# Sums of four of v moved from TensorE to GpSimd in a planned attention and MoE kernel, and a later due time for the second batch's units

## The chip, the cores and the metric

One core of one Trainium2 chip runs the whole program. The metric is the device time of one execution in microseconds (us), as the median of several runs. Lower is better.

## The reference

q, k and v are (8 batches, 8 heads, 576 rows, 64 columns). For each batch and head there are two attentions, whose results are added:

```
q_d, k_d, v_d = means of 4 neighbouring rows of q, k, v     # 144 rows
out_up    = repeat(softmax(q_d @ k_d.T / 8) @ v_d, 4 times each row)
out_local = softmax(mask(|i - j| < 4, q @ k.T / 8)) @ v
x   = (out_up + out_local), as 4608 tokens of 512 numbers
h   = x @ w_in                       # 512 -> 2048
out = (h * clip(h + 3, 0, 6) / 6) @ w_out
```

So before the large matrix products can use a batch, the kernel needs that batch's sums of four rows of v: 144 of them for each head, 128 from v's first 512 rows and 16 from its last 64.

## The kernel before

**Units.** A unit is two heads of one batch (128 columns), so a batch `b` has four units, numbered `hp` 0 to 3. A unit loads q and k, has them transposed, sums groups of four (`pool4`, L323), makes the scores of both attentions (`scores_d` L419, `scores` L601), the two softmaxes (maximum L470, subtraction L473, exponential L463 and L476, sum L479, reciprocal L485, normalisation `norm` L487 to L492), transposes the weights (`trans_d` L496 with L501, `trans` L632 with L638), copies them out of PSUM (L120 on ScalarE, L122 on VectorE) and multiplies with v (`pv_d` L575 with L586 and L589, `pv` L646 with L656). Normalisation is usually GpSimd's.

**Chunks.** The tokens go through the two large products in chunks (`PART`): 512 tokens first, then 256, then 384 at a time. For each of 16 blocks `f` of the hidden width a first product (`gemm1`, L934) is followed by an activation (ScalarE L940, VectorE L944), a split into two rounded halves (L948, L952) and a second product (`gemm2`, L986). x itself is split in two halves too (L122 or L120, then L837). Chunk 0 is batch 0's first 512 rows; chunk 1 is the rest of batch 0 and the start of batch 1; chunk 2 is all batch 1.

**Batch 0 is direct.** For `b == 0` (`direct`) both attentions are accumulated in PSUM, in two banks for each unit, and x is split straight out of these banks. All of batch 0's banks (`s`) come from six. Its q and k are transposed on TensorE (L274). Each unit's first 512 rows of v arrive in one load (`ld4(0)`, L362), and `sum_pe(0)` (L386) sums them by four matmuls with the identity matrix into one bank (L393); a copy (`evict_v`, L395, by L120 or L122) takes the sums to SBUF. The last 64 rows are summed by one matmul with a 0/1 matrix (L391). Batch 1 (`alone` but not `direct`) already has the first 512 rows summed by `sum4` (L370): one reduction on VectorE (L376), or two additions on GpSimd (L378, L379).

**Weights.** The weights come as 64-bit numbers and are made into two rounded float halves, with ScalarE (L180, L195, L201), VectorE (L185, L189) and either VectorE or GpSimd (L205); a weight's load is L169.

**The order.** All operations are entered into a planner (`Plan`), which simulates the engines at assumed costs before anything is emitted. Each operation has a due time `late`, worked back from deadlines; an engine that is free takes the ready operation with the earliest `late` whose buffers and banks are free. The result is one fixed order for each engine and for SP's queue of loads. `on("sum4", 1.0)` offers VectorE at 1.03 us and GpSimd at 1.3 us, and `PEN["sum4"]` counts GpSimd's offer as due 10 us sooner. Where the planner sees TensorE idle ahead of the first large product, it puts in matmuls that compute nothing (`busy`, L1033, with L1038).

The due time of a batch's units comes from

```
def need(b):
    return start_of(need_chunk(b)) - (EARLY * TC if b and b % 2 == 0 else 0.0) - SLACK[min(b, 3)]
```

and each earlier unit of batch 1 is due 22 (`UNIT_T[1]`) sooner than the next. Everything that batch 1's units do (loads L311, transposes L318, `pool4` L327 or L331 and L333, and all that follows) inherits its `late` from there.

Of the kernel before, what the change touches and what calls it, by code (L numbers as in the profile page):

```python
# [56 lines left out]
def tile_local_down_attention_moe(ctx, tc, q_all, k_all, v_all, _qk_loc, _v_loc, w_in, w_out, ident_d, _mask_d, out):  # L57
# [26 lines left out]
    op = plan.op  # L84
# [74 lines left out]
    def plan_weights(n, keys, after, gate):  # L159
# [43 lines left out]
        def lo(eng):  # L203
# [5 lines left out]
               for i in range(nk)]  # L209
        a = op("ACT", 0.2 + cols / 1070, rebias, lds, take=[place], lag=LAGW)  # L210
        c = op("ACT", 0.2 + cols / 1070, low, lds, lag=LAGW)
        b = op("DVE", 0.2 + cols / 930, partial(bits, 0), [a, c], lock=not by_bank)
# [22 lines left out]
    def plan_duo(b, d, masked):  # L235
# [50 lines left out]
        for u in range(2):  # L286
            unit = plan_unit(b, d, u, row0, k0, kv, PS, qk, evicts, users, masked, early_user, due - (1 - u) * unit_time(b))
            next(unit)
            units.append(unit)
            if b < ALONE or len(units) > 1:  # L290
                next(units.pop(0), None)
# [4 lines left out]
    def plan_unit(b, d, u, row0, k0, kv, PS, duo, evicts, users, masked, early_user, due):  # L296
        hp = 2 * d + u
        row0 = row0 + u * S
        un = b, hp
# [3 lines left out]
        alone = b < ALONE  # L303

        direct = b == 0
# [29 lines left out]
        for kind, t in (("q", q_all), ("k", k_all)):  # L335
# [3 lines left out]
            else:  # L339
                rk = "raw" + k0, hk  # L340
                l = op("SP", 2.0, partial(ldt, t, kind), loads if b == 1 else [], take=[rk], size=dma(4 * S, 128), nd=4)
# [59 lines left out]
        lv, sums = [], []  # L401
# [4 lines left out]
        for g in range(2):  # L406
            rk = ("raw4", ("v", un)) if b == 0 else ("raw" + k0, ("v", un, g))
            l = op("SP", 0.5, partial(ld4, g), take=[rk], size=dma(P, 512) if alone and g else dma((P, NAR)[g], 2048), nd=1 if alone else 1 + g)
            if b == 0:
                loads.append(l)  # L410
            if b == 0 or alone and g:
                bk = PS, ("v4", un, g)
                a = early_user(op("PE", 0.21 if g else 0.86, partial(sum_pe, g), [l], take=[bk], free=[rk], lag=LAGT, rec=2 if g else 8))
                sums.append(early_user(op(on("ev", ROW), 0, partial(evict_v, g), [a], take=[("vd" + k0, un)], free=[bk])))
            else:
                sums.append(op(on("sum4", 1.0), 0, partial(sum4, g), [l], take=[("vd" + k0, un)], free=[rk]))


        def scores_d():  # L419
# [275 lines left out]
        else:  # L695
# [3 lines left out]
                take=[bk, pk, sk] + bks + [pl, sl], lag=LAGT, rec=52)  # L699
# [20 lines left out]
        if alone:  # L720
            subs = []
            for g in range(2):
                a = op("DVE", 0.45, lambda g=g: top(rows(g), greatest(g)), [sl_op])
                subs.append(op("DVE", 0.45, lambda g=g: minus(nc.vector, st["p"][:, :, g], rows(g), greatest(g)), [a],
                               free=[bks[g]]))
# [41 lines left out]
        else:  # L767
            rk = "qk", ("rd", un)
# [7 lines left out]
        else:  # L776
            a = op("PE", 1.4, pv_all, t + lv + turned_d + sums, take=bks + [ok] + xbs,
                   free=[tk, vk, tk_d, ("vd" + k0, un)], lag=LAGT, rec=52)
# [280 lines left out]
    for n in range(len(PART)):  # L1059
        while duos and (need_chunk(duos[0][0]) == n or units):  # L1060
            b, d = duos.pop(0)
# [9 lines left out]


T0, TC, TF, LAG = 55.0, 82.0, 5.1, 2
UNIT_T, EARLY, SLACK = (4.0, 22.0, 20.0, 30.0), 0.7, (4.0, 40.0, -5.0, 28.0)
PRE, GATE = 4, 14

AHEAD = 2
# [14 lines left out]
LAGT = 0.5  # L1092

LAGW = 2.0
ORDERED = ("raw", "qk", "qkd", "v", "vd", "P", "Pd", "Pl", "PT", "rl", "od", "p4", "st", "a", "o0", "o1", "o2", "o3")
HOP, FREE = 0.1, 0.1

# [96 lines left out]
def on(what, size):  # L1194

    return {e: (a + b * size, PEN[what].get(e, 0.0)) for e, (a, b) in COST[what].items()}
# [19 lines left out]
def dma(packets, size):  # L1216

    return packets * (6.5 + 0.049 * size) / 16e3 if size > 256 else packets * (1.3 + 0.13 * size) / 16e3


class Plan:
# [5 lines left out]
    def op(self, eng, cost, fn, after=(), take=(), free=(), size=0, dl=None, lag=0.0, lock=False, rec=0, nd=1, kind=None):  # L1227
        o = Op(len(self.ops), eng, cost, fn, take, size, dl)
        o.kind = kind

        o.rec, o.nd = rec, nd
        o.lag, o.lock = lag, {True: ("DVE", "POOL"), False: ("POOL",)}[lock]
        self.ops.append(o)
        for a in after:
            self.dep(o, a)
        for r in free:
            self.free_after(r, [o])
        return o
# [28 lines left out]
    def emit(self, warm, last, busy):  # L1267
# [30 lines left out]

        turn = {key: [] for key in ORDERED}

# [214 lines left out]
```

## Time and profile before

| what | us |
|---|---|
| median of 3 runs | 946.02 |
| lowest and highest of them | 945.36 and 947.41 |
| the profiled execution's own time | 944.02 |
| its span, first to last instruction | 942.2 |
| TensorE busy in the span | 931.6 |
| VectorE, ScalarE, GpSimd busy | 554.2, 363.2, 298.8 |

PE is TensorE's matmuls, PEld its weight loads, DVE is VectorE, ACT ScalarE, POOL GpSimd, SPq the queue in which SyncE issues transfers. Each engine runs its instructions in the emitted order, and waits at the first that isn't ready. In the timelines the time in brackets is how long the engine stood idle before that row, and for whom it waited.

### The profile page before, as it was taken

To read this page: it belongs to the slowest core of one execution; us is meant where nothing else is said; L and a number is where in the kernel's file an instruction comes from. 1 tells how busy PE (TensorE), PEld (TensorE's weight loads), DVE (VectorE), ACT (ScalarE), POOL (GpSimd) and SP (SyncE) were. 2 spreads that over 40 slices of the span, in tenths; PEclk is the share of its full clock that TensorE was granted. 3 is DMA by queue.
4 is the path that set the end of the run, shared out by engine and by line. 5 is a ranking of instruction groups with operands and counts; after the bars stand their busy time and mean duration, and the time that the engine had idled before them with its cause. 6 is when DMAs were issued, how large, how long until landed. Compare 5 with 4: busy or idle time off the path is not lost.

```text
span 942.2 us, 19819 instructions
## 1 busy us (share of the span) xinstructions
PE 931.6 (99%) x7567; PEld 808.5 (86%) x7567; DVE 554.2 (59%) x1045; ACT 363.2 (39%) x899; POOL 298.8 (32%) x386
## 2 busy tenths in 40 slices
PE   8999999999999999999999999999999999999997
PEld 5677778988889898889889888988988988998996
DVE  7888886477677566554456667555455654323322
ACT  5787755334333334333233333333233432221222
POOL 4345361244462334332325244225125320000000
PEclk9999999999999999999999999999999999999999
DMA  7999353355666565545135555645154520100101
GB/s 210 228 293 288 72 118 64 70 105 119 126 134 132 104 117 113 100 84 114 34 80 122 102 104 102 134 98 97 40 99 80 115 55 12 34 1 2 33 1 33
DMA packets 311758, 93.52 MB, mean 99 GB/s; under 512 B 251376, under 2 KB 297840, under 8 KB 311664
## 3 DMA queue, kind: packets, MB, share of 16 engines
q1 hardware_dynamic: 311376, 91.83, 43.8%
q8 instruction: 59, 0.97, 0.4%
q10 hardware_dynamic: 288, 0.43, 0.2%
q14 instruction: 35, 0.29, 0.1%
HBM read 69.60 MB, written 22.61 MB: 98 GB/s over the span
## 4 chain that ended last, share of the span: by engine, by line
PE 90%; SPq 4%; DMA 3%; DVE 1%; issue 1%; ACT 1%; POOL 0%; DVEq 0%; ACTq 0%
PE h L934 40%; PE o L986 39%; PE a L656 2%; PE a L615 2%; PE a L442 1%; PE a L986 1%; PE a L570 1%; SPq L311 1%; DMA rows<-in_k_dram 1%; DMA arena<-in_v_dram 1%; SPq L548 1%; PE a L428 1%; SPq L522 1%; SPq L527 1%; DMA arena<-in_q_dram 0%
## 5 line engine op out<-in xcount | busy, mean ns | idle before, releaser
L934 PE MATMUL h<-rounded,wp 128*128 128x384 f32 (+2 forms) x2240 | 420.1, 336 | 0.2 <-DVE arena L944 0.2
L986 PE MATMUL o<-wp,rounded 128*128 128x512 f32 x1680 | 408.1, 394 | 0.0
L934 PEld LDWEIGHTS h<-rounded,wp 128*128 128x128 f32 x2240 | 384.1, 188 | 15.1 <-issue 2.7
L986 PEld LDWEIGHTS o<-wp,rounded 128*128 128x128 f32 x1680 | 311.0, 188 | 66.1 <-issue 4.4
L940 ACT ACTIVATE arena<-h 128x384 f32<-128x384 f32 (+2 forms) x192 | 93.7, 490 | 365.6 <-PE h L934 364.7
L944 DVE SCALAR_TENSOR_TENSOR arena<-arena,h 128x384 f32<-128x384 f32 (+2 forms) x192 | 105.1, 547 | 183.0 <-ACT arena L940 181.8
L948 ACT CAST rounded<-arena 128x384 fp32r<-128x384 f32 (+2 forms) x192 | 98.2, 512 | 119.2 <-DVE arena L944 118.7
L952 DVE TENSOR_TENSOR rounded<-arena,rounded 128x384 fp32r<-128x384 f32 (+2 forms) x136 | 79.9, 588 | 78.3 <-PE o L986 42.9
L952 POOL TENSOR_TENSOR rounded<-arena,rounded 128x384 fp32r<-128x384 f32 (+2 forms) x56 | 62.5, 1118 | 156.3 <-ACT rounded L948 102.9
L331 POOL TENSOR_TENSOR arena<-arena 128x144 f32<-128x144 f32 x36 | 16.2, 450 | 182.6 <-PE a L442 101.5
L318 DVE STREAM_TRANSPOSE arena<-arena 128x576 f32<-128x576 f32 x56 | 43.1, 772 | 24.1 <-PE a L615 11.4
L492 POOL TENSOR_TENSOR arena<-arena 128x640 f32<-128x640 f32 (+1 forms) x34 | 41.7, 1227 | 20.0 <-DVE arena L485 15.9
L333 POOL TENSOR_TENSOR arena<-arena 128x144 f32<-128x144 f32 x72 | 41.1, 570 | 5.6
L837 POOL TENSOR_TENSOR rounded<-arena,rounded 128x384 fp32r<-128x384 f32 (+1 forms) x10 | 15.0, 1511 | 71.2 <-ACT rounded L120 70.9
L473 POOL TENSOR_TENSOR arena<-arena 128x640 f32<-128x640 f32 x21 | 26.5, 1264 | 27.7 <-DVE arena L470 17.1
L376 DVE TENSOR_REDUCE arena<-arena 128x128 f32<-128x512 f32 (+1 forms) x28 | 30.0, 1071 | 8.8 <-PE a L570 6.9
L463 ACT ACTIVATE arena<-a,arena 128x144 f32<-128x144 f32 x84 | 31.5, 379 | 1.7
L536 DVE STREAM_TRANSPOSE arena<-arena 128x384 f32<-128x384 f32 (+1 forms) x48 | 21.5, 462 | 16.9 <-DMA arena<-pd 15.0
L205 POOL TENSOR_TENSOR wp<-early,wp 128x1024 fp32r<-128x1024 f32 (+1 forms) x9 | 19.4, 2158 | 34.4 <-ACT wp L201 34.4
L615 PE MATMUL a<-arena 64*64 64x64 f32 x1220 | 30.0, 223 | 0.0
L470 DVE TENSOR_REDUCE arena<-a 128x1 f32<-128x144 f32 (+2 forms) x65 | 26.1, 410 | 4.6 <-PE a L615 2.9
L656 PEld LDWEIGHTS a<-arena 64*64 64x64 f32 x1120 | 19.1, 134 | 9.5 <-issue 7.9
(186 smaller groups left out, 808.9 us busy)
## 6 DMA issues: line engine op xcount, KB each, us to landing
rawp<-in_w_in_dram SPq DMA_DIRECT2D x16, 512.0 KB
rawp<-in_w_out_dram SPq DMA_DIRECT2D x16, 512.0 KB
arena<-in_q_dram SPq DMA_DIRECT2D x112, 72.0 KB
arena<-in_k_dram SPq DMA_DIRECT2D x112, 72.0 KB
pl<-arena SPq DMA_DIRECT2D x24, 320.0 KB
arena<-pl SPq DMA_DIRECT2D x96, 80.0 KB
arena<-in_v_dram SPq DMA_DIRECT2D x28, 256.0 KB
out_dram<-arena SPq DMA_DIRECT2D x91, 72.0 KB
```

The lines of the kernel that those rows point to most:

```text
L318: nc.vector.transpose(out=qk[kind], in_=st["raw", kind].rearrange("p j i -> p (j i)"))
L333: eng.tensor_tensor(t, t, x[:, :, r], op=ALU.add)
L463: nc.scalar.activation(p[:, j], x[:, j], AF.Exp, bias=m[:, j:j + 1], scale=1.0 / 128.0, accum_out=s[:, j:j + 1])
L492: eng.tensor_tensor(x, x, s.unsqueeze(2).broadcast_to(list(x.shape)), op=ALU.mult)
L615: nc.tensor.matmul(st["ps", g][half:half + WIN, jj * D:jj * D + WIN], qk_of("q")[hs, k_first:k_first + WIN], qk_of("k")[hs, k_first:k_firs ...
L656: nc.tensor.matmul(st["px"][g][h * D:(h + 1) * D, at + lo:at + hi], st["v"][ks, jj, h * D:(h + 1) * D], st["pt"][ks, jj, half + lo:half + ...
L934: nc.tensor.matmul(st["ps"], win[f][:, wt, kk * P:(kk + 1) * P], xs[part][:, kk], start=(kk == 0 and i == 0), stop=(kk == NK - 1 and i == ...
L940: nc.scalar.activation(st["t"], st["ps"], AF.Relu, bias=3.0)
L944: nc.vector.scalar_tensor_tensor(out=t, in0=t, scalar=6.0, in1=st["ps"], op0=ALU.min, op1=ALU.mult)
L948: nc.scalar.copy(st["gh"], st["t"])
L952: eng.tensor_tensor(st["gl"], st["t"], st["gh"].bitcast(F32), op=ALU.subtract)
L986: nc.tensor.matmul(otile[n, m], gt[:, ms], wout[f][:, wt], start=(f == 0 and i == 0), stop=(f == NF - 1 and i == 2),)
```

## The change

`SUMMED` lists the units of batch 0 whose first 512 rows of v go through `sum4` instead of `sum_pe`: all four. For them GpSimd alone is offered. The sums of the last 64 rows stay on TensorE. `SLACK[1]`, which batch 1's due times are worked out from, falls from 40 to 32.

```
-            if b == 0 or alone and g:
+            if b == 0 and (g or hp not in SUMMED) or alone and not direct and g:
                 bk = PS, ("v4", un, g)
                 a = early_user(op("PE", 0.21 if g else 0.86, partial(sum_pe, g), [l], take=[bk], free=[rk], lag=LAGT, rec=2 if g else 8))
                 sums.append(early_user(op(on("ev", ROW), 0, partial(evict_v, g), [a], take=[("vd" + k0, un)], free=[bk])))
             else:
-                sums.append(op(on("sum4", 1.0), 0, partial(sum4, g), [l], take=[("vd" + k0, un)], free=[rk]))
+                sums.append(op({"POOL": on("sum4", 1.0)["POOL"]} if direct else on("sum4", 1.0), 0, partial(sum4, g), [l], take=[("vd" + k0, un)], free=[rk]))
...
-UNIT_T, EARLY, SLACK = (4.0, 22.0, 20.0, 30.0), 0.7, (4.0, 40.0, -5.0, 28.0)
+UNIT_T, EARLY, SLACK = (4.0, 22.0, 20.0, 30.0), 0.7, (4.0, 32.0, -5.0, 28.0)
...
+SUMMED = 0, 1, 2, 3
```

## Rows read from the trace of the kernel before

**Rows 1.** The page: its first line, and the busy time of the engines.

```profile
span 942.2 us, 19819 instructions
PE 931.6 (99%) x7567; PEld 808.5 (86%) x7567; DVE 554.2 (59%) x1045; ACT 363.2 (39%) x899; POOL 298.8 (32%) x386
```

**Rows 2.** Waits of PE, first 70 us: line, releaser, us in total, times, longest.

```profile
PE o L638 <- DVE arena L122: 0.4, 1, 0.4
PE h L934 <- DVE arena L944: 0.2, 1, 0.2
```

**Rows 3.** Waits of PE, from 70 us to the end.

```profile
PE a L656 <- ACT arena L463: 0.4, 1, 0.4
```

**Rows 4.** Chain of waits, 17 to 24 us: start, us, what.

```profile
17.64 1.09 PE o L393 x8
...
23.10 0.89 PE a L393 x8
```

**Rows 5.** Timeline of PE: the matmuls that compute nothing, and the first large product.

```profile
20.98 1.25 PE L1038 MATMUL h<-identb 128*128 128x512 bf16 x5
...
30.45 1.04 PE L1038 MATMUL h<-identb 128*128 128x512 bf16 x4
...
38.13 0.59 PE L1038 MATMUL h<-identb 128*128 128x512 bf16 x2
...
42.50 0.50 PE L934 MATMUL h<-rounded,wp 128*128 128x512 f32 x1
```

**Rows 6.** Timeline of POOL: a sum of batch 1, and the longest later one.

```profile
58.66 0.75 POOL L378 TENSOR_TENSOR arena<-arena 128x256 f32<-128x256 f32 x1
59.48 0.46 POOL L379 TENSOR_TENSOR arena<-arena 128x128 f32<-128x128 f32 x1
59.91 3.53 POOL L952 TENSOR_TENSOR rounded<-arena,rounded 128x512 fp32r<-128x512 f32 x2
...
516.39 1.42 POOL L378 TENSOR_TENSOR arena<-arena 128x256 f32<-128x256 f32 x1
```

**Rows 7.** Timeline of POOL, 19 to 37 us: normalisations.

```profile
19.14 0.91 POOL L492 TENSOR_TENSOR early<-early,arena 128x432 f32<-128x432 f32 x1 [1.55 <-DVE arena L485]
...
26.89 0.91 POOL L492 TENSOR_TENSOR early<-early 128x432 f32<-128x432 f32 x1 [2.52 <-DVE early L485]
...
34.30 2.48 POOL L492 TENSOR_TENSOR early<-early 128x640 f32<-128x640 f32 x2
```

**Rows 8.** Busy time of POOL alone, 17.6 to 36.8 us: length, busy time.

```profile
17.60:36.80 19.20, 11.04 (x15) 1.00 0.93 243
```

**Rows 9.** Timeline of DVE, 29 to 36 us: batch 1's work.

```profile
29.02 0.78 DVE L318 STREAM_TRANSPOSE arena<-arena 128x576 f32<-128x576 f32 x1 [1.43 <-DMA arena<-in_k_dram]
...
31.70 0.78 DVE L318 STREAM_TRANSPOSE arena<-arena 128x576 f32<-128x576 f32 x1 [0.54 <-DMA arena<-in_k_dram]
...
34.20 1.05 DVE L376 TENSOR_REDUCE arena<-arena 128x128 f32<-128x512 f32 x1
```

**Rows 10.** Timeline of SP's queue, 23 to 28 us: batch 1's first loads.

```profile
23.32 2.39 SPq L311 DMA_DIRECT2D arena<-in_q_dram  x4
25.80 2.34 SPq L311 DMA_DIRECT2D arena<-in_k_dram  x4
```

**Rows 11.** Busy times by stretch: us, then PE, PEld, DVE, ACT, POOL, clock, DMA.

```profile
30.00:42.50 12.50, 11.95 (x150) 6.24 (x148) 11.60 (x23) 8.82 (x21) 5.53 (x7) 1.00 1.06 302
...
58.00:100.00 42.00, 41.95 (x317) 32.56 (x318) 37.27 (x52) 34.41 (x61) 20.44 (x18) 1.00 0.85 254
```

**Rows 12.** Timeline of DVE where chunk 1's x is split.

```profile
150.15 1.51 DVE L837 TENSOR_TENSOR rounded<-arena,rounded 128x384 fp32r<-128x384 f32 x4
```

**Rows 13.** Timeline of PE where chunk 1 begins.

```profile
153.15 1.60 PE L934 MATMUL h<-rounded,wp 128*128 128x256 f32 x12
154.58 2.23 PE L986 MATMUL o<-wp,rounded 128*128 128x512 f32 x9
...
157.33 1.60 PE L934 MATMUL h<-rounded,wp 128*128 128x256 f32 x12
```

## The prediction

> **What bounds the kernel now.** I read the busy times first: TensorE works in 931.6 of 942.2 us, and the next engine, VectorE, in 59% of them [rows 1]. A busy engine can still be stalled between instructions, so the list of TensorE's waits comes next. Between 14 and 70 us it shows 0.4 us for a copy and 0.2 us for a gate [rows 2]; from 70 us to the end 0.4 us [rows 3]. From the first large product on, at 42.5 us [rows 5], TensorE is thus a queue that never runs dry. The time is a sum: when that stream starts, plus all its work, plus the stalls within it. A microsecond taken off TensorE ahead of the stream counts in full, if the stream can start that much sooner; a microsecond taken off another engine counts only if TensorE had been waiting for it.
>
> So the question is what holds TensorE between 13 and 42.5 us. It looks full there too, but three groups of matmuls that compute nothing stand in it, 1.25, 1.04 and 0.59 us, 2.9 in all [rows 5]: the planner expected waits there. That stretch is partly bound by TensorE and partly by chains through the other engines. From 30 us on VectorE is nearly full as well, 11.60 of 12.5 us [rows 11].
>
> A note on the sum: the profiled execution took 944.02 us, 1.8 more than its span and 2.0 less than the median, 946.02. I work out a difference and apply it to the median. A measurement of this kernel can tell about 0.2% from no change, 1.9 us.
>
> **The sums on TensorE go.** Each unit of batch 0 has four matmuls with the identity, eight records in the trace. In the chain of waits two of the four groups take 1.09 and 0.89 us of TensorE's time [rows 4]. The mean is 0.99 us, and four times that 4.0 us; the bounds, from the shorter and the longer, are 3.6 and 4.4 us. Four copies out of PSUM go too, on VectorE or ScalarE, and four takings of one of six banks. Those are off the path unless a bank was what TensorE waited for; the 1.25 us of idle matmuls at 21 us stand where sums of unit 0, scores of units 2 and 3 and others hold banks, so some of it may go as well.
>
> **The sums on GpSimd come.** Batch 1's first unit shows the same instructions in the same shapes: from the start of the first addition at 58.66 us to the start of the next operation at 59.91 us are 1.25 us [rows 6]. Four make 5.0 us, between 17.6 and 36.8 us mostly. There GpSimd works 11.0 of 19.2 us [rows 8], so 8.2 us are free, and longer waits of 1.55 and 2.52 us stand ahead of normalisations [rows 7]. The cover is there in total, but not always at the right moment. The sums count as due 10 us sooner, so a sum that is ready goes ahead of a normalisation, and behind the normalisations are TensorE's transposes and products with v. The new wait is that of `pv_d` for GpSimd, and that of GpSimd for the load of v: GpSimd stands in order, so a load later than the planner thinks also holds the normalisation behind it. The trace of before shows no sum of batch 0 on GpSimd. Its cost to TensorE lies between nothing (all four in gaps) and 5.0 us (each delays a normalisation by its whole length, and nothing covers it). I take one collision on the path, 1.25 us. It is nearer the lower end because the free time exceeds the work and TensorE has other units' work to take in between.
>
> A rule bears on this price. The longest first addition of a later batch took 1.42 us where the first took 0.75 us [rows 6], so something slows GpSimd at times. The Trainium skill, "SBUF — State Buffer", section "Who interferes with whom", says that a VectorE instruction with two SBUF inputs shuts out a GpSimd instruction that reads SBUF, and the other way round, for the whole instruction. By it a sum that met such an instruction would cost more than 1.25 us. VectorE's work from 17 to 30 us is mostly reductions, reciprocals and PSUM copies, and the neighbouring normalisations of one shape all take 0.91 us [rows 7], so I keep the short price and make the long one a rival.
>
> **Batch 1's units are due 8 us later.** `start_of(1)` is 55 + 82 x 512/384 = 164.3 on the planner's clock, so the due time of the last unit goes from 124.3 to 132.3 and that of the first from 58.3 to 66.3. The number of operations stays the same on every engine. What moves is the order, starting with SP's queue: eight descriptors for q and k of batch 1's first unit take 4.7 us [rows 10] between the first and the second weight, and some weights will go ahead of them. On VectorE the first unit's two transposes wait 1.43 and 0.54 us for these loads, with batch 0's reciprocals and copies queued behind them, and a sum of batch 1 follows [rows 9]: 2.0 us of waiting and 0.78 + 0.78 + 1.05 = 2.6 us of work, 4.6 us in all, in the stretch where VectorE was full. Moved behind, they let VectorE keep pace with a TensorE that is 4 us ahead. On TensorE and GpSimd the same unit's work only changes places with large products. I cost this part at nothing of its own: it is what lets the 4.0 us through. Its cover afterwards is VectorE's free time between 58 and 100 us, 42.0 - 37.3 = 4.7 us [rows 11], which would take the 2.6 us.
>
> **The sum.** -4.0 for the matmuls, +1.25 for one collision, 0 for the later units: -2.75 us, from 946.02 to about 943.3 us. The stalls in the stream, 0.2 and 0.4 us [rows 2, 3], are left as they are.
>
> **The rivals.**
>
> More comes off. If the freed banks and the freed VectorE also make the idle matmuls unnecessary, up to 2.9 us [rows 5] go besides. With all of them and no collision that is 4.0 + 2.9 = 6.9 us, 939.1 us; with half and no collision, 5.4 us, 940.6 us. For it: a tight bank count at 21 us. Against: two of the three groups stand ahead of transposes that wait for softmax and copies, not for a sum.
>
> Nothing comes through. The chain through VectorE and GpSimd sets the start of the stream, and the 4.0 us become waits or idle matmuls: 946.0 us, with 944.2 to 947.0 around it (947.0 if all four collide, -4.0 + 5.0). For it: VectorE at 93% from 30 us [rows 11] and the 2.9 us that TensorE already idles. Against: 4.6 us of VectorE's load there are batch 1's.
>
> Slower: chunk 1 waits for batch 1. The place is where chunk 1's x is split. The last low halves end at 150.15 + 1.51 = 151.7 us [rows 12] and the first product on them starts at 153.15 us, a margin of 1.5 us. Behind it two second products of chunk 0, 157.33 - 154.58 = 2.75 us each, are left to put in front [rows 13], 5.5 us. Together 7.0 us. TensorE 2.75 us early uses up some of that, leaving 4.3 us; if the last unit comes more than 4.3 us later in absolute time, TensorE stalls. At 8 us later the stall is 3.7 us: 943.3 + 3.7 = 947.0 us. If the first unit's loads also fall behind weights for the length of their issue, 4.7 us [rows 10], it is 8.4 us: 951.7 us. The middle, 949.4 us, is its price. For it: the units follow one another through single buffers, so a delay of the first may reach the last. Against: from the second unit on they are behind their due times (the last due at 124.3, its results used at 150), so a later due time need not move them.
>
> The long price on GpSimd. By rows alone: if the sum on the path takes 1.42 - 0.75 = 0.67 us more in its first addition, and as much in its second, it costs 2.6 us, and the time is 944.6 us. The rule of the Trainium skill named above would do this here.
>
> **How the numbers follow.** One collision or so, 943.3 us: 0.46. More comes off, 940.6 us: 0.12. Nothing comes through, 946.0 us: 0.22. Chunk 1 waits, 949.4 us: 0.14. The long price, 944.6 us: 0.06. The first two are faster by over 0.2% (below 944.1 us): 0.58. The third and the fifth are within 0.2%: 0.28. The fourth is slower (above 947.9 us): 0.14. The range has to reach over the third case's upper end, 947.0 us, and down into the second to 939.8 us, which leaves out most of the fourth and a little of the second. The likeliest case's own range, with removed work of 3.6 to 4.4 us and zero to two collisions, is 941.6 to 944.9 us.
>
> **What would show it.** In the changed profile L393 is gone, and L378 and L379 stand four times between 15 and 32 us at about 0.75 and 0.46 us. TensorE's first L934 starts 2 to 4 us before 42.5 us, and everything after keeps that distance up to the end. VectorE's first L318 comes after 35 us, with no wait of over 1 us. The idle matmuls stay near 2.9 us; if they grow by the 4 us taken away, the second rival holds. A wait of TensorE for L837 near 150 us is the third. The prediction is wrong if the first L934 starts sooner and the distance is lost later, or if L492 of units 1 to 3 comes later than before.

## The result and the profile after

The changed kernel takes 947.83 us, the median of 14 runs, beside 945.72 us for 14 runs of the kernel before on the same chip: a ratio of 1.0025 [1.0015, 1.0034] (in brackets the 95% interval, here and below). The change costs 2.1 us where 2.7 were to be gained, and the time lies outside the predicted range. The profiled execution took 949.21 us, 1.4 more than its median; that of before was 1.7 below 945.72. So the two traces lie 5.2 us apart, and the sums below are made against that.

The page, its first line and the busy times, to be read beside [rows 1]:

```profile
span 947.4 us, 19744 instructions
PE 933.1 (98%) x7541; PEld 807.0 (85%) x7541; DVE 561.9 (59%) x1052; ACT 359.7 (38%) x888; POOL 296.1 (31%) x387
```

TensorE is busy for longer, 933.1 us after 931.6, although its 16 identity matmuls are gone. A busy time that grows while work is taken away means that something was slower, or that matmuls without a result were added; here it is both.

The waits of TensorE, whole span, where before the longest behind 14 us was 0.4 us [rows 2, 3]:

```profile
PE o L391 <- DMA early<-in_v_dram: 3.0, 1, 3.0
...
PE h L934 <- DVE arena L944: 1.5, 1, 1.5
...
PE a L656 <- ACT arena L463: 0.4, 1, 0.4
```

The first is new, and the second was 0.2 us. The first is not a wait for GpSimd's sums: L391 is what stayed on TensorE, the sum of a unit's last 64 rows, and it waits for its load. The timeline of TensorE shows where:

```profile
20.27 0.39 PE L391 MATMUL a<-early,four 64*16 64x128 f32 x2
20.76 0.37 PE L391 MATMUL o<-early,four 64*16 64x128 f32 x2
21.06 1.04 PE L1038 MATMUL h<-identb 128*128 128x512 bf16 x4
25.10 0.58 PE L391 MATMUL o<-early,four 64*16 64x128 f32 x2 [3.00 <-DMA early<-in_v_dram]
...
28.90 3.60 PE L589 MATMUL o<-arena 128*64 128x288 f32 x16
...
43.96 0.48 PE L934 MATMUL h<-rounded,wp 128*128 128x512 f32 x1
...
49.70 2.32 PE L589 MATMUL a<-early 128*64 128x288 f32 x16
```

Three L391 come close together now, and the last is the fourth unit's. Before the change it stood at 30.13 us, behind all four groups of identity matmuls, and its load had landed by then. Behind the wait 16 matmuls of L589 take 3.60 us, where another unit's 16 take 2.32 us further on. Why, the table of stretches says (length, then busy time of PE, PEld, DVE, ACT, POOL, then TensorE's granted clock, DMA share, GB/s):

```profile
20.00:25.10 5.10, 2.00 (x33) 0.77 (x26) 2.77 (x10) 1.96 (x8) 2.29 (x4) 0.97 0.72 195
25.10:28.90 3.80, 3.80 (x51) 2.47 (x51) 1.72 (x3) 2.07 (x9) 2.51 (x5) 0.50 1.24 278
28.90:32.50 3.60, 3.60 (x21) 1.48 (x18) 2.62 (x8) 1.36 (x4) 1.61 (x2) 0.62 1.19 195
32.50:42.50 10.00, 9.93 (x128) 6.01 (x130) 7.88 (x15) 7.27 (x16) 6.28 (x9) 1.00 1.02 379
```

TensorE did 2.00 us of work in 5.1 us, and then ran at the lower of its two levels, 0.50 (1.2 of 2.4 GHz), for 3.8 us and partly for 3.6 more. Against full speed that costs 3.80 x 0.50 + 3.60 x 0.38 = 3.3 us. In this execution the stall is paid about twice. The clock fell in the others too: its mean over a whole run is 0.997 in the median of the 14 runs of the changed kernel, and 0.999 in that of 23 runs of the kernel before (those timed with the first four experiments). On 933 us that makes 1.9 us, an estimate from rounded clocks.

VectorE stands as long as TensorE, since its copy of that sum waits for L391, and batch 0's softmax stands behind the copy:

```profile
25.72 0.28 DVE L122 COPY early<-o 16x128 f32<-16x128 f32 x1 [2.95 <-PE o L391]
25.93 0.80 DVE L479 TENSOR_REDUCE arena<-early 128x10 f32<-128x640 f32 x1
```

The loads themselves, in SP's queue, are as late as they were:

```profile
20.56 0.58 SPq L362 DMA_DIRECT2D early<-in_v_dram  x1
21.19 0.49 SPq L364 DMA_DIRECT2D early<-in_v_dram  x1
...
23.59 2.43 SPq L311 DMA_DIRECT2D arena<-in_q_dram  x4
...
35.36 8.87 SPq L311 DMA_DIRECT2D arena<-in_q_dram  x4
```

L364 brings the fourth unit's last 64 rows. It is issued at 21.2 us in both kernels; in the planner's simulation it is issued at 15.1 and has landed at 19.6 us. Before, the planned place of its L391 was 28.7 us on that same clock, and an error of some 5 us didn't show. With the identity sums gone and the order drawn anew the planned place is 21.1 us, and it does. Note also L311: the loads of batch 1's first three units stand behind 2, 10 and 22 loads of weights, where they stood behind 1, 7 and 18, and start at 23.59, 35.36 and 65.34 us, where they were at 23.32 [rows 10], 33.15 and 58.65:

```profile
33.15 6.15 SPq L311 DMA_DIRECT2D arena<-in_q_dram  x4
...
58.65 5.80 SPq L311 DMA_DIRECT2D arena<-in_q_dram  x4
```

GpSimd's timeline in the same stretch:

```profile
20.52 0.72 POOL L378 TENSOR_TENSOR early<-early 128x256 f32<-128x256 f32 x1 [1.03 <-DMA early<-in_v_dram]
...
24.85 0.72 POOL L378 TENSOR_TENSOR early<-early 128x256 f32<-128x256 f32 x1 [2.21 <-DMA early<-in_v_dram]
25.65 0.46 POOL L379 TENSOR_TENSOR early<-early 128x128 f32<-128x128 f32 x1
26.06 0.91 POOL L492 TENSOR_TENSOR early<-early,arena 128x432 f32<-128x432 f32 x1
```

Each sum costs what batch 1's did [rows 6], 1.2 us. The fourth waits 2.21 us for its load, with a normalisation behind it: the collision that the prediction had looked for, beside the one that it had not.

Last, VectorE where the second new wait of TensorE ends, the 1.5 us for the gate L944 at 60 us:

```profile
58.40 0.89 DVE L470 TENSOR_REDUCE arena<-a 128x5 f32<-128x320 f32 x2 [0.17 <-PE a L615]
59.20 0.88 DVE L473 TENSOR_TENSOR arena<-a,arena 128x320 f32<-128x320 f32 x2
60.00 0.16 DVE L485 RECIPROCAL arena<-arena 128x3 f32<-128x3 f32 x1
60.08 0.66 DVE L944 SCALAR_TENSOR_TENSOR arena<-arena,h 128x512 f32<-128x512 f32 x1
```

A softmax of batch 1 stands ahead of the gate on which the large product waits.

**The account.** The last second product (L986) starts at 929.07 us before and at 934.19 us after, 5.1 us later. From 13 us on, idle time of TensorE rises from 1.2 to 5.1 us, +3.9. The lower clock costs 3.3. The matmuls that compute nothing rise from 11 (2.9 us by their rows [rows 5]) to 17; a further one in a row costs 0.22 us (1.04 - 0.59 us, for two more), so +1.3. That is 8.5 us, and the end is only 5.1 later: the real work has shrunk by 3.4 us, by subtraction. In the timeline of before the four groups of L393 take 1.09, 0.89, 0.99 and 0.89 us, each from its start to that of the next instruction, 3.9 in all. The 4.0 us did go, to within half a microsecond.

### The profile page after: what moved, and what is told of

Read it like the earlier page. It is cut to its first block, busy times and chain, and to the rows that moved or that the text cites. A ratio compares the mean times of both kernels' runs of the same rounds, so it can differ in the third digit from the quotient of the medians.

```text
span 947.4 us, 19744 instructions
## 1 busy us (share of the span) xinstructions
PE 933.1 (98%) x7541; PEld 807.0 (85%) x7541; DVE 561.9 (59%) x1052; ACT 359.7 (38%) x888; POOL 296.1 (31%) x387
## 4 chain that ended last, share of the span: by engine, by line
PE 94%; SPq 2%; DMA 2%; DVE 0%; issue 0%; ACT 0%; POOL 0%; ACTq 0%
PE h L934 42%; PE o L986 41%; PE a L656 2%; PE a L615 2%; PE a L442 1%; PE a L570 1%; PE a L986 1%; DMA arena<-in_v_dram 1%; PE o L589 1%; PE a L501 1%; PE a L638 1%; SPq L351 1%; PE a L589 0%; DMA early<-in_v_dram 0%; PE a L428 0%
## 5 line engine op out<-in xcount | busy, mean ns | idle before, releaser
L934 PE MATMUL h<-rounded,wp 128*128 128x384 f32 (+2 forms) x2240 | 420.4, 336 | 1.5 <-DVE arena L944 1.5
L986 PE MATMUL o<-wp,rounded 128*128 128x512 f32 x1680 | 408.6, 394 | 0.0
L934 PEld LDWEIGHTS h<-rounded,wp 128*128 128x128 f32 x2240 | 383.9, 188 | 17.2 <-issue 2.4
L986 PEld LDWEIGHTS o<-wp,rounded 128*128 128x128 f32 x1680 | 310.8, 188 | 65.5 <-issue 3.8
L944 DVE SCALAR_TENSOR_TENSOR arena<-arena,h 128x384 f32<-128x384 f32 (+2 forms) x192 | 104.9, 546 | 184.9 <-ACT arena L940 183.9
L952 POOL TENSOR_TENSOR rounded<-arena,rounded 128x384 fp32r<-128x384 f32 (+2 forms) x55 | 59.4, 1080 | 160.6 <-ACT rounded L948 101.2
L331 POOL TENSOR_TENSOR arena<-arena 128x144 f32<-128x144 f32 x35 | 15.7, 449 | 183.0 <-PE a L442 113.8
L318 DVE STREAM_TRANSPOSE arena<-arena 128x576 f32<-128x576 f32 x56 | 43.0, 770 | 25.1 <-PE a L615 11.7
L492 POOL TENSOR_TENSOR arena<-arena 128x640 f32<-128x640 f32 (+1 forms) x33 | 40.2, 1219 | 23.2 <-DVE arena L485 16.5
L333 POOL TENSOR_TENSOR arena<-arena 128x144 f32<-128x144 f32 x70 | 39.7, 567 | 5.5
L837 POOL TENSOR_TENSOR rounded<-arena,rounded 128x384 fp32r<-128x384 f32 (+2 forms) x12 | 16.3, 1372 | 73.6 <-ACT rounded L120 71.0
L615 PEld LDWEIGHTS a<-arena 64*64 64x64 f32 x1220 | 26.1, 135 | 2.0 <-issue 1.6
L205 POOL TENSOR_TENSOR wp<-early,wp 128x1024 fp32r<-128x1024 f32 (+1 forms) x7 | 17.4, 2485 | 31.7 <-ACT wp L201 31.7
L656 PEld LDWEIGHTS a<-arena 64*64 64x64 f32 x1120 | 19.1, 134 | 9.5 <-issue 7.5
```

What stands on the lines that cost most here:

```text
L318: nc.vector.transpose(out=qk[kind], in_=st["raw", kind].rearrange("p j i -> p (j i)"))
L333: eng.tensor_tensor(t, t, x[:, :, r], op=ALU.add)
L492: eng.tensor_tensor(x, x, s.unsqueeze(2).broadcast_to(list(x.shape)), op=ALU.mult)
L615: nc.tensor.matmul(st["ps", g][half:half + WIN, jj * D:jj * D + WIN], qk_of("q")[hs, k_first:k_first + WIN], qk_of("k")[hs, k_first:k_firs ...
L656: nc.tensor.matmul(st["px"][g][h * D:(h + 1) * D, at + lo:at + hi], st["v"][ks, jj, h * D:(h + 1) * D], st["pt"][ks, jj, half + lo:half + ...
L934: nc.tensor.matmul(st["ps"], win[f][:, wt, kk * P:(kk + 1) * P], xs[part][:, kk], start=(kk == 0 and i == 0), stop=(kk == NK - 1 and i == ...
```

## The experiments

The records name the theories by letters. **A**: TensorE's wait at the fourth unit's L391, with the lower clock behind it, is the loss. **B**: the later due time of batch 1 is. **C**: GpSimd's wait at its fourth sum is. **E**: each stall that is taken away comes back as another further on. Ratios are against the kernel before on the same chip.

**The two parts alone.** First, the sums as changed, the due time as before (the diff is against the changed kernel, as all that follow unless they say otherwise).

```
-UNIT_T, EARLY, SLACK = (4.0, 22.0, 20.0, 30.0), 0.7, (4.0, 32.0, -5.0, 28.0)
+UNIT_T, EARLY, SLACK = (4.0, 22.0, 20.0, 30.0), 0.7, (4.0, 40.0, -5.0, 28.0)
```

> The sums of batch 0's first 512 rows on GpSimd, batch 1's due time as before (SLACK 40). Theory A (late load): the changed kernel loses where TensorE's last L391 stands 3.0 us for a load of v that lands at 25 us, and in the stretch at a lower granted clock behind it; that comes with the sums, whatever the due time. It expects a wait of 2 to 4 us at L391, a granted clock below 0.9 from 20 to 33 us, and 947 to 949 us. Theory B (later units): the sums save their 4.0 us and the later due time loses 6 by crowding the gates of the first chunk. It expects 942 to 943 us and no wait over 0.5 us at L944.

957.12 us, ratio 1.0132 [1.0105, 1.0159]: 12 us slower than before, and no theory's number. B is the further off, as it has the sums alone gain 3 us. Its waits:

```profile
PE h L934 <- DVE arena L944: 6.2, 3, 3.1
...
PE o L391 <- DMA early<-in_v_dram: 1.8, 1, 1.8
```

The wait for the load is there, and shorter. Gates of the large product now come three times behind other work of VectorE. Then the due time as changed, the sums as before (against the kernel before):

```
-UNIT_T, EARLY, SLACK = (4.0, 22.0, 20.0, 30.0), 0.7, (4.0, 40.0, -5.0, 28.0)
+UNIT_T, EARLY, SLACK = (4.0, 22.0, 20.0, 30.0), 0.7, (4.0, 32.0, -5.0, 28.0)
```

> The sums on TensorE as before, batch 1's units due later (SLACK 32). A: no wait at L391 over 0.5 us, clock 1.00, 944 to 946.5 us. B: the loss of 6 us without the 4.0 us of gain, 949 to 952 us, with waits of TensorE at L944 or L837.

952.77 us, 1.0084 [1.0059, 1.0109], just over B's range and far from A's. Here no L391 waits, nor any L944 or L837, but TensorE's timeline has this at the start of chunk 1, and the table of stretches (PE alone, then the clock) the price:

```profile
154.38 1.44 PE L656 MATMUL a<-arena 64*64 64x60 f32 x40 [2.54 <-DVE arena L122]
156.88 0.79 PE L986 MATMUL o<-wp,rounded 128*128 128x512 f32 x1 [1.06 <-ACT wp L201]
158.24 3.78 PE L986 MATMUL o<-wp,rounded 128*128 128x512 f32 x8 [0.56 <-POOL wp L205]
```

```profile
150.00:160.00 10.00, 5.25 (x56) 0.67 0.49 98
160.00:170.00 10.00, 10.00 (x53) 0.81 0.41 82
```

4.75 us idle and some 3.6 more by the clock (5.25 x 0.33 + 10 x 0.19), at the third rival's place, in a kernel that it wasn't written for. The longest wait is in a unit's product with v; the other two are for halves of weights. Alone, the parts cost 12 and 7 us; together, 2. They don't add, because each is an input to one plan, and each plan draws the order anew over the first 160 us.

**The wait and the clock apart.** Fourteen matmuls that compute nothing go ahead of the L391 that waits, so that TensorE stands idle no longer but gets nothing done sooner either.

```
+                a.pad = 14 if direct and g and hp == 3 else 0; ...
...
-            if o.busy:
-                busy(o.busy)
+            if o.busy + o.pad:
+                busy(o.busy + o.pad)
```

> The changed kernel, with 14 more matmuls that compute nothing (0.22 us each, 3.0 us) in front of the L391 that stood for its load; the order of everything else is the same. A: TensorE isn't idle there and the granted clock stays at 1.00; the load still lands at 25 us, but what follows from 25.1 to 32.5 us, at 0.50 and 0.62 in the changed kernel, runs at full clock. Time granted away there: 3.8 x 0.50 + 3.6 x 0.38 = 3.3 us, so 944.0 to 945.5 us. If the clock is only an accompaniment and a chain through GpSimd and VectorE sets the start of the stream (theory C), the matmuls only get shorter and waits take their place: 947 to 948.5 us.

946.66 us, 1.0018 [1.0004, 1.0032]; the wait at L391 is 0.3 us, the granted clock 1.00 throughout that stretch, and the first L934 starts at 41.17 us, 2.8 sooner than in the changed kernel. From its first L428 to its last L986 the profiled execution takes 917.2 us, that of the changed kernel 920.3: the clock's part of the loss is back. The median lies between the two theories' ranges, so it shows a part of that, at the edge of what it can tell.

**The load in time.** The loads of v for batch 0 are entered with the earliest due time, so that each unit's v is issued ahead of the two loads that it had stood behind (L351, L355); first in the changed kernel, then, as a control, in the kernel before.

```
-l = op("SP", 0.5, partial(ld4, g), take=[rk], size=dma(P, 512) if alone and g else dma((P, NAR)[g], 2048), nd=1 if alone else 1 + g)
+l = op("SP", 0.5, partial(ld4, g), take=[rk], size=dma(P, 512) if alone and g else dma((P, NAR)[g], 2048), nd=1 if alone else 1 + g, dl=0.0 if b == 0 else None)
```

> The changed kernel, with the loads of v that are summed (L362, L364) issued for all four units ahead of those that are only multiplied (L351, L355). A: no unit's sum waits for its load, neither on TensorE nor on GpSimd; no wait over 0.5 us at L391 or L378, granted clock 1.00, and both the 3.0 us of wait and the 3.3 us of clock come back: 941 to 943.5 us. C (the sums on GpSimd hold the normalisations by their own length, loads or not): the first large product stays near 44 us and the time at 946 to 948 us.

> The kernel before, with the loads of v that are summed issued ahead of those that are only multiplied: a control for the loads-first run. Theory A says that before the change no sum waited for its load, so an earlier load gives nothing: 944 to 947 us, waits of TensorE under 1 us each. If the order of the loads is worth something by itself (theory D: what the loads-first run gained came from elsewhere), it is faster by the 2 to 3 us that the same edit gave the changed kernel: 942 to 943.5 us.

945.34 us, 1.0006 [0.9988, 1.0024], and for the control 944.93 us, 0.9992 [0.9981, 1.0004]. The move does nothing for the kernel before, and the wait at L391 is gone from the changed one, whose first L934 now starts at 40.53 us. The loss is undone, but A's gain (941 to 943.5 us) hasn't come. A new wait of 2.3 us stands near 62 us. VectorE, GpSimd and TensorE there:

```profile
57.10 3.40 DVE L185 SCALAR_TENSOR_TENSOR early<-rawp 128x1024 int32<-128x1024 int32 x1
```

```profile
55.62 3.80 POOL L205 TENSOR_TENSOR wp<-early,wp 128x512 fp32r<-128x512 f32 x2
```

```profile
64.29 1.10 PE L986 MATMUL a<-wp,rounded 128*128 128x512 f32 x3 [2.26 <-DVE wp L205]
```

The same L185 takes 1.22 us at 70.51 us. At 57.10 us it met GpSimd's two subtractions (L205) and ended a microsecond after them. VectorE has no idle time from there to the weight half (L205, 63.62 us) for which TensorE waits, so the 2.2 us arrive there; no run takes them away to show it.

**The order alone.** Next, nothing is re-planned; single operations of the changed kernel move in the finished order (by a helper that isn't shown: what waits for them moves along). The fourth unit's L391 goes three of TensorE's operations later; GpSimd's fourth sum goes two of its operations later; both.

```
+SINKS = [('sum_pe', ('s', ('v4', (0, 3), 1)), 3)]
```

> The changed kernel in its own order, but for one operation: the fourth unit's L391 (with the four idle matmuls ahead of it and the copy behind it) stands three TensorE operations later, behind L501 of the first unit and the scores L607, L615 of the fourth. Theory A: the scores run in the time that was waited; the wait at L391 falls from 3.0 to under 1 us, the granted clock stays at 1.00, VectorE's softmax of the fourth unit starts 3 to 6 us sooner; 943.5 to 945.5 us. If GpSimd's wait for the same load (2.2 us at L378, with a normalisation behind it) sets what comes next, theory C, most of it is lost again at L501 or L589: 946.5 to 948 us.

```
+SINKS = [('sum4', ('vd0', (0, 3)), 2)]
```

> The changed kernel in its own order, but the fourth unit's sum on GpSimd (L378, L379) stands two GpSimd operations later, behind the second unit's normalisation; L391 stays. Theory A: TensorE still stands at L391 for 2 to 3 us and the clock still falls; 947 to 948.5 us. Theory C: the normalisations come 3 us sooner and the time falls to 944 to 945.5 us.

> Both moves together. Theory A: as with the L391 moved alone, within 1 us. If both waits hold the same chain, only this one gains: 942.5 to 944.5 us, with neither of the two gaining alone.

With L391 later: 946.43 us, 1.0008 [0.9994, 1.0022], clock 1.00. With GpSimd's sum later: 950.67 us, 1.0053 [1.0033, 1.0073]. With both: 946.97 us, 1.0016 [1.0007, 1.0026]. The first is over A's range and no clear gain by itself, as its interval overlaps that of the changed kernel (1.0015 to 1.0034), yet GpSimd still waits 3.1 us for the load in it. The second only shortens GpSimd's wait, from 2.2 to 1.4 us, but the normalisation that had stood behind it starts over 2 us sooner, and the kernel got slower, which nothing here explains. C, which expects the time to come back with the normalisation, falls; TensorE's wait is left. In the table of stretches of that kernel the lower clock is still there, because L391 still waits (2.5 us):

```profile
25.00:30.00 5.00, 3.60 (x50) 0.59 0.97 215
30.00:35.00 5.00, 5.00 (x40) 0.72 0.83 138
```

**Both waits.** The changed kernel was timed again beside one in which that L391 goes three operations later and the first gate (L944) goes ahead of five operations of VectorE.

```
+SINKS = [('sum_pe', ('s', ('v4', (0, 3), 1)), 3)]
+HOISTS = [('gate', 5)]
```

> The changed kernel itself once more, on the chip of the three runs beside it, for a closer comparison: 947 to 949 us, a wait of 2 to 3.5 us at L391 and a granted clock below 0.9 from 20 to 33 us.

> The kernel with only the last sum L391 moved (946.4 us), with the first gate L944 also moved, ahead of five VectorE operations of batch 1's first unit (two L470, two L473, one L485). TensorE waited 1.5 us for that gate. Theory A: that wait falls below 0.4 us and the time to 944 to 945.5 us. Theory E: another wait takes its place, 946 to 947.5 us.

The changed kernel: 948.4 us, 1.003 [1.0014, 1.0046], with a wait of 3.6 us at L391. The lower clock behind it is shorter than in the first profile (PE alone, then the clock), and costs 4.56 x 0.34 = 1.6 us where it cost 3.3:

```profile
25.00:30.00 5.00, 4.56 (x58) 0.66 1.14 260
30.00:35.00 5.00, 5.00 (x39) 1.00 1.11 221
```

The other: 945.43 us, 0.9999 [0.9986, 1.0012], the first L934 at 39.53 us, and waits for L944 of 0.6 us in two. On one chip, two moves in an otherwise equal order take 3.0 us off and undo the whole loss. The waits did cost it.

**Half of the sums.** `SUMMED = 0, 1`, with the later due time:

> The changed kernel with only the first two units' sums on GpSimd (SUMMED = 0, 1); the third and the fourth keep theirs on TensorE, which stand in front of the last L391 and give its load time to land. Theory A: no wait over 1 us at L391, clock 1.00 from 20 to 33 us, and with 2.0 us of TensorE's work gone 943.5 to 945.5 us, unless a stall elsewhere is new. If what the planner does with the later due time decides (theory B), it is as slow as that alone: 950 to 954 us.

945.35 us, 0.9997 [0.9983, 1.0012], in A's range and not in B's. L391 doesn't wait; half of the matmuls are gone and no gain can be told.

**Where the gain stays.** Two more kernels ask for it: the loads ahead, with the one L205 that TensorE waited for raised past four of VectorE's operations; and the kernel with both moves, without the matmuls that compute nothing behind 15 us.

```
+RAISED = [4]
```

> The loads-first kernel in its own order, with the single L205 on VectorE that frees the fourth output bank raised ahead of four VectorE operations (two L318 and L327 of batch 1's second unit, one L485); nothing else moves. Theory A (the 4.0 us are there, single stalls eat them): TensorE's wait at L986 falls from 2.3 to under 1 us, the granted clock from 58 to 70 us returns from 0.86 to over 0.95, and of 2.3 + 1.7 us some 2 to 4 come back: 941.5 to 943.5 us. Theory E (every stall taken away comes back as another): 944.5 to 946.5 us.

```
-            if o.busy:
+            if o.busy and o.start < 15.0:
```

> The kernel with L391 and the gate moved (945.4 us), without the 17 matmuls that compute nothing after the first 15 us. They take 3.7 us of TensorE, 1.3 more than before the change. If TensorE would do real work in their place (theory F: they now eat part of the gain), 942.5 to 944.5 us. If they only fill waits (theory A), waits of the same length stand in their place and the time is the same, 944.5 to 946.5 us, or over 946.5 us where such a wait lowers the granted clock.

The first: 945.52 us, 0.9996 [0.9982, 1.001]. The wait for L205 falls to 0.2 us, and two of 2.0 us in all for L944 stand in its place, as E has it; the clock from 58 to 70 us stays at 0.86. Its first L934 starts at 38.35 us, 4.2 sooner than before, and the time is the same: from there to the last L986 it takes 892.1 us, before 886.6, because 3.2 us more of idle time and 1.4 of lower clock (10.11 x 0.14) lie behind it. The start of the first L934 alone doesn't tell the end. (An earlier form of this move, with what waits for the moved operations carried along, computes other values than the reference; in it a transpose L318 waited 11.3 us for its load and TensorE 13.1 us for one L944, so its 958.07 us say nothing on the question.) The second: 945.95 us, 1.0005 [0.9992, 1.0018]. Its clock:

```profile
20.00:25.00 5.00, 3.22 (x54) 0.84 0.76 206
25.00:30.00 5.00, 4.54 (x18) 0.50 0.93 217
30.00:35.00 5.00, 5.00 (x28) 0.63 0.90 259
```

Without them the first L934 starts at 42.62 us, 3.1 later than with them, but the time can't be told from the one with them (0.9999). They hold the clock, and they don't eat the gain; that they pay isn't shown. The same edit on the first of the two kernels:

> The raised kernel without the matmuls that compute nothing after 15 us (9 of them, 1.9 us). Theory F: 1 to 2 us faster than the raised kernel. Theory A: the same within 0.7 us, or slower by 1 to 3 us if a wait lowers the granted clock.

945.72 us, 1.0014 [0.9998, 1.003], with a clock of 0.54 from 35 to 42.5 us.

**The sums alone, with the loads in time.** The loads ahead, and the due time as before:

```
-UNIT_T, EARLY, SLACK = (4.0, 22.0, 20.0, 30.0), 0.7, (4.0, 32.0, -5.0, 28.0)
+UNIT_T, EARLY, SLACK = (4.0, 22.0, 20.0, 30.0), 0.7, (4.0, 40.0, -5.0, 28.0)
```

> The loads-first kernel with batch 1's due time as before (SLACK 40): the sums alone, with loads in time. Theory A: the run of the sums alone (957.1 us) lost at three gates L944, 6.2 us, not at a load; the due time is what the later units are for, so the gates are late here too: 948 to 956 us, waits at L944 of over 3 us. If the late load had set off the rest: 942 to 946 us.

> The same kernel as the one with the loads ahead and the sums alone (943.7 us, ratio 0.9985 with an interval of 0.9970 to 0.9999), timed again, since the interval only just left out 1. If the sums pay once their loads are in time, the ratio is again 0.997 to 0.9995, 1 to 3 us under the kernel before. If that was chance, it is 0.9995 to 1.002, as in the other kernels with the loads ahead.

943.7 us, 0.9985 [0.997, 0.9999], and again 943.81 us, 0.9988 [0.9973, 1.0003]. It is the fastest kernel of the study. The second interval takes in 1. The kernel was timed again because its first ratio, the lowest so far, only just left out 1, so that ratio may flatter it. Taken as independent, their mean is 0.9987 with an interval narrower by the root of two, some 0.0010 to each side: 1.3 us (0.3 to 2.3) under the kernel before, less than the 1.9 us that the prediction held to be measurable. By A it should have been slower, like the sums alone: a miss, and a telling one. The 12 us that the sums alone lost hang on the loads of v and on the plan that follows from them, which is the only difference between the two kernels; and the later due time isn't needed for this result.

The two profiles of that kernel have spans of 939.9 and 944.1 us, and the largest single difference on the way to the first L934 is in TensorE's timeline at 30 us. In the first:

```profile
30.71 0.49 PE L501 MATMUL a<-ident,early 128*16 128x128 f32 x3 [1.18 <-DVE early L122]
...
31.35 0.71 PE L589 MATMUL a<-early 128*64 128x288 f32 x4
```

In the second:

```profile
32.26 0.81 PE L501 MATMUL a<-ident,early 128*16 128x128 f32 x3 [1.73 <-DVE early L122]
...
33.42 1.24 PE L589 MATMUL a<-early 128*64 128x288 f32 x4
```

The same wait, 0.55 us longer, is followed by L589 at 1.24 us in place of 0.71: the lower clock again. The first L934 starts at 37.77 and at 40.69 us. So one kernel has two outcomes 2.9 us apart by then: 1.0 us was there before this wait (0.4 of it from the start, the rest from two short waits), 0.55 us is the wait, and 1.4 us come behind it, where the clock is lower.

## Why the prediction was wrong

**What bounds the kernel: right.** TensorE's queue sets the end, and what its stalls cost could be read there, stall by stall.

**The sums on TensorE, -4.0 us: right.** The rows of all four groups add up to 3.9 us, within the bounds, and the account finds 3.4 us of work gone.

**The sums on GpSimd, 1.25 us each: right in price** (0.72 and 0.46 us to run, no long one), so the rival of the long price did not come, and the trace has no case of the Trainium skill's rule ("SBUF — State Buffer", "Who interferes with whom") at these sums. The kernel with the loads ahead has one that agrees with it, elsewhere: VectorE's L185, which reads SBUF twice, took 3.40 us for 1.22 beside GpSimd's L205, which reads SBUF.

**The step that failed** is the new wait: "The new wait is that of `pv_d` for GpSimd, and that of GpSimd for the load of v". It was priced at one collision, 1.25 us. GpSimd did wait for that load, 2.21 us, and to let the normalisation go first gained nothing. The wait that decided was TensorE's own, 3.0 us at the L391 that the change leaves alone. The prediction had seen that a load later than the planner thinks holds up an engine that stands in order, and asked it of the engine that gets work. It had not asked it of the engine that loses work, whose next instruction moves up. The trace of before held a part of the number: L364 issued at 21.2 us, and its L391 at 30.1 us with the identity sums in front of it that were to go. Without these 4 us alone it would have come at some 26 us, still behind the landing at 25; that the new order puts it at 21 on the planner's clock can be seen only in the new plan. Nor was there a term for the clock, 3.3 us, as the trace of before has no stall of that length behind 14 us.

The prediction's own second sign of being wrong was there: the four L492 of 128x432 start at 21.74, 26.06, 26.65 (on VectorE) and 32.11 us, where they were at 19.14, 22.10, 22.97 and 26.89 us. The first is late by the sums that go ahead of it on GpSimd, the others by the wait as well.

**The later units, 0 us: wrong in size and in reason.** The first L318 came at 34.58 us without a wait, and the loads L311 fell behind weights, both nearly as foretold. But VectorE's softmax of batch 1 came to stand ahead of the first gates (1.5 us; the sums alone, with the due time as before, wait 6.2 us there, so it isn't shown that the due time does it). And the later due time does not "let the 4.0 us through": alone it costs 7 us, and the best version does without it. Beside the sums with their late loads it is worth 9 us (957.1 to 947.8): its price hangs on the plan that it meets.

**The rivals.** "Chunk 1 waits" named the right sign for a reason that didn't occur: in the changed kernel there is no wait for L837 and none of over 0.4 us behind 70 us, although the fourth unit's loads start 11 us later (89.52 for 78.40). That 947.8 lies in its span, 947.0 to 951.7 us, is luck. "Nothing comes through" ends at 947.0; of its mark, idle matmuls that grow by 4 us, 1.3 were there. "First L934 2 to 4 us before 42.5" failed at once: 43.96 us.

**What stays open.** In the fastest version 1.3 us (0.3 to 2.3) of the 4.0 come through. Its first profile has no lower clock and no more idle matmuls than before, and TensorE's idle time behind 14 us is 3.1 us where it was 1.2: of 3.9 us that leaves 2.0, and from the first L428 to the last L986 it is 1.7 us shorter (913.3 for 915.0). Its second profile has longer waits and the lower clock, and is 2.2 us longer. What decides between the two isn't settled. Nor is it settled operation by operation why the sums alone, without the loads ahead, come out 12 us slower, as their plan differs in too many places.

## What to carry to other kernels

Where work is taken off the engine that sets the time, look at the instruction that moves up into its place, and at when its inputs really land in the trace, not in the plan: a planner that is 5 us early on one load is harmless for as long as something stands in front of it. Price a stall on TensorE by its length and by the matmuls behind it at the lower clock; in two profiles of the changed kernel these added 3.3 us to a stall of 3.0, and 1.6 to one of 3.6. In a kernel whose order a planner draws, the parts of a change don't add, so each is timed with the others present.

## What the runs showed of the hardware

After idle stretches TensorE's granted clock fell to its lower level for some microseconds: 0.50 and 0.62 over 7.4 us behind the 3.0 us at L391, and 0.66 over 5.0 us behind 3.6 us at the same L391 in another execution, so the longer stall had the smaller price. In two executions of one kernel the same matmuls took 0.71 us behind a wait of 1.18 us at L501, and 1.24 us behind one of 1.73 us. Fourteen more matmuls that compute nothing kept the clock at 1.00 over the gap at L391, where it fell to 0.50 without them.

An integer operation of VectorE (L185, 128x1024) took 3.40 us beside two subtractions of GpSimd, and 1.22 us later on: 2.2 us, with a wait of 2.3 us on TensorE behind them.
